# Attention, Mish MLP and SwiGLU MLP in one kernel: another order of work in the attention blocks at its start

## Chip, cores and metric

The kernel runs on one core of a Trainium2 chip. The metric is the device time of one execution in microseconds (us); a time quoted for a version is the median of several runs.

## The reference, cut to what matters

```python
# q, k, v: (4, 8, 576, 64)
scores = np.matmul(q, k.transpose(0, 1, 3, 2)) / np.sqrt(D)
# heads 0 to 3: the 32 positions up to the own one; heads 4 to 7: every 32nd position up to the own one
attn = softmax(np.where(mask, scores, -1e9))
x = np.matmul(attn, v)  # as (2304 tokens, 512)
h = x @ w_in            # 512 -> 2048
x = (h * np.tanh(softplus(h))) @ w_out
x = (silu(x @ w_gate) * (x @ w_val)) @ w_out2   # 512 -> 1536 -> 512
```

The weights come as 64-bit floats and are made into 32-bit ones on the chip.

## The kernel before, in words

**Attention** is cut into 24 steps: 4 batches, in each 3 steps of local heads (8 or 6 small score tiles of 64 queries by 96 keys) and 3 of strided heads (8 or 6 tiles of 64 by 64). One call of `at_pair` issues one *block*: parts of four steps at once, by the table `PAIR` of (function, lag). Block a holds, in the order of the table: loads (`at_load`), the transposes of step a-2 (`at_tr`, PE, line L394) with their copy out of PSUM (`at_copy`, first half on DVE, L404, second on ACT, L402), the sum's small addition and the normalisation of step a-1 (`at_add`, `at_norm`: POOL L374 and L382, DVE reciprocal L379), the product with v of step a-3 (`at_pv`, PE, L423), its split into a high part on ACT (`at_hi`, L81) and a low part on DVE (`at_lo`, L86), the scores of step a (`at_qk`, PE, L322), their masked maximum on DVE (`at_max`, L347) and their exponentials on ACT (`at_exp`, L363). The result of attention, x, lies in five chunks of 512 tokens as a pair `xh`, `xl`. Blocks are counted from 0; blocks 0 to 14 are issued by one loop, the later ones inside the matmuls of the MLP, at the places `PAIR_AT`.

**Between blocks** the loop issues, for block k: `KEEP[k]` idle matmuls on zeros (`spin`, L830), `WSTEPS[k]` steps of weight conversion, and the matmul steps `GROUPS[k]` of the first MLP. A step (n, f, kc) is three matmuls of 512 columns into PSUM tile f of chunk n, from slice kc of x: high by high, high weight by `xl`, low weight by high (`mm3`, L90; PE tile `h`). Slice kc belongs to head pair kc, so a slice becomes ready in the block whose `at_pv` finishes that pair.

**A weight tile** takes four conversion steps on DVE (L214, L217, L220, L223) and a square on ACT (L213) in between. When the four are done, the next block's `at_whi` rounds the high part on ACT (L81, tile `w`), and `at_wlo` at the end of that block takes the low part on DVE (L86, tile `w`). The third conversion step frees the raw buffer (two of them), so that the next raw tile can be loaded (`w_load`, 512 KB).

**Order.** Each engine takes its instructions in the order in which the code issues them. SP issues the loads in that order too. A load on the SP and ACT queues waits until the eighth one before it has landed.

Of the kernel before, what the change touches and what calls it, by code (L numbers as in the profile page):

```python
# [7 lines left out]
F32 = mybir.dt.float32  # L8
# [18 lines left out]
QW = S + 16  # L27
KW = S + STR
# [24 lines left out]
}  # L53
WSTEPS = (0, 0, 4, 0, 2, 2, 4, 2, 2, 2, 2, 2, 2, 2, 2)
WFILL = 4
PAIR_AT = (0, 13, 16, 19, 22, 25, 28, 31, 35, 40, 45, 49)
WF = 8
DO2 = 6

# [2 lines left out]
def local_strided_attention__mish_moe__swiglu_kernel(  # L62
# [10 lines left out]
    nc = tc.nc  # L73
    small = ctx.enter_context(tc.tile_pool(name="small", bufs=1))
    sb = ctx.enter_context(tc.tile_pool(name="sb", bufs=1))
# [9 lines left out]
    def split_lo(eng, lo, src, hi):  # L85
        eng.tensor_tensor(out=lo, in0=src, in1=hi.bitcast(F32), op=ALU.subtract)  # L86
# [10 lines left out]
    xh, xl, acc = {}, {}, {}  # L97
# [35 lines left out]
    def w_load():  # L133
        i = wpos[0]
        while i < len(wlist) and wlist[i][1] is None:
            i += 1
        if i >= late["first"] and late["raw"] is None:
            return
        if i < len(wlist):
            if i < late["first"]:  # L140
                raws[i] = sb.tile([128, 512], I64, tag="raw", name="raw", bufs=2)
            else:
                raws[i] = late["raw"][:, late["loads"] % 2]
                late["loads"] += 1
            nc.sync.dma_start(raws[i], wlist[i][1])
        wpos[0] = i + 1
# [124 lines left out]
    pairs = []  # L271
    steps, at_first, at_last = [], {}, {}
    for b in range(B):
        for first in (0, 2) if b < B - 1 else (2, 0):
# [18 lines left out]
    qk_t, v_t = {}, {}  # L293
    st = {}

    def load_qk(i, cuts=((0, QW + KW),)):
        b, hp = pairs[i]
        a = QK_SLOT[i]
        t = sb.tile([128, QW + KW], F32, tag=f"acc{a}", name="qk")
        for c0, c1 in cuts:  # L300
            nc.sync.dma_start(t[:, c0:c1], qk[4 * b + hp, :, c0:c1])
        qk_t[i] = t

    def load_v(s):
        b, first, g, part = steps[s]
        n = len(part) // 2
        k = 128 if first else LK
        t = sb.tile([128, 2, 4, 128], F32, tag="v", name="v", bufs=2)[:k, :, :n]
        src = (v_str if first else v_loc)[b, 2 * g:2 * g + 2, :, :n]
        nc.sync.dma_start(t, src.rearrange("x p n d -> p x n d"))  # L310
        for x in range(2):
            v_t[s, x] = t[:, x]
# [155 lines left out]
    def at_wlo(s):  # L468
        w_lo(nc.vector)
# [4 lines left out]
    def of(do, h):  # L474
        return lambda s: do(s, h)

    PAIR = [
        (at_load, 0),
        (of(at_tr, 0), -2),
        (of(at_copy, 0), -2),  # L480
        (at_add, -1),
        (at_norm, -1),
        (at_pv, -3),
        (at_v, -3),
        (at_hi, -3),
# [9 lines left out]
        (at_wlo, 0),  # L495
    ]
    SPLIT, EXP0, COPY1, EXP1 = 9, 11, 15, 16
    apos = [0]

    rest = []  # L500

    def at_rest():
        while rest:
            rest.pop(0)()

    def at_pair(split=False, later=()):
        at_rest()
        a = apos[0]
        if a < NS + 3:
            apos[0] += 1  # L510
            for x, (do, lag) in enumerate(PAIR):
                if 0 <= a + lag < NS:
                    if x in later:
                        held.append(lambda do=do, s=a + lag: do(s))
                    elif split and x >= SPLIT:
                        rest.append(lambda do=do, s=a + lag: do(s))
                    else:
                        do(a + lag)
# [303 lines left out]
    with tc.manual_schedule():  # L822
        nc.gpsimd.memset(wz, 0.0)

        def spin(n):
            if not n:
                return
            wp = ps.tile([128, 512], F32, tag="mm", name="wp", bufs=3)
            for _ in range(n):
                nc.tensor.matmul(  # L830
                    wp, lhsT=wz[:, :128], rhs=wz.unsqueeze(1).to_broadcast([128, 2, 256]), start=True, stop=True
                )

        spin(NWARM)
        load_qk(0, ((QW, QW + 416),))
        nc.scalar.dma_start(qk_t[0][:, :384], qk[0, :, :384])
        nc.scalar.dma_start(cst[:, :192], consts[:, :192])
        load_qk(1, ())
        nc.scalar.dma_start(qk_t[1][:, :192], qk[1, :, :192])
        for i, c0, c1 in ((0, 384, QW), (0, QW + 416, QW + KW), (1, QW, QW + 224)):  # L840
            nc.sync.dma_start(qk_t[i][:, c0:c1], qk[i, :, c0:c1])
        nc.sync.dma_start(cst[:, 192:], consts[:, 192:])
        w_load()
        for c0, c1 in ((192, QW), (QW + 224, QW + KW)):
            nc.sync.dma_start(qk_t[1][:, c0:c1], qk[1, :, c0:c1])
        load_v(0)
        load_qk(2)
        load_v(1)
        load_qk(3)
        w_load()  # L850
        nc.scalar.preload_act_table_set(EXP)

        NA = NQ * NCH
# [7 lines left out]

        for k in range(len(WSTEPS)):
            at_pair()
            spin(KEEP.get(k, 0))
            w_step(WSTEPS[k])
            for x in GROUPS.get(k, ()):
                g1_step(*x)
                if x == (1, 0, 3):
                    for f in range(QF):
                        act_m(0, (f,))  # L870
                        g_hi(0, f)
        MISH = (
            (lambda: act_m(1, (0, 1, 2)), lambda: g_lo(0, 0)),
            (lambda: g_lo(0, 1),),
            (lambda: g_lo(0, 2),),
            (),
            (lambda: at_wlo(0), lambda: g_lo(0, 3), lambda: w_step(WFILL), lambda: act_m(1, (3,)), act_m_end),
        )
# [3 lines left out]
        def fill():  # L882
            at_rest()
            if fills[0] in PAIR_AT:
                at_pair(apos[0] >= NS, () if fills[0] else LATER)
            for x in MISH[fills[0]] if fills[0] < len(MISH) else ():
                x()
            fills[0] += 1
            do(3 if len(todo) > 10 else 2 if len(todo) > DO2 else 1)

        g1s = [(1, 3, kc) for kc in range(4)]
        g1s += [(2, f, kc) for kc in range(4) for f in range(3)] + [(2, 3, kc) for kc in range(4)]
        wfill = [0]
        for n in range(1, 3):
# [16 lines left out]
        while apos[0] < NS + 3:  # L911
            at_pair()
# [177 lines left out]
```

## Time and profile before

| what | value |
| --- | --- |
| time, median of 3 runs | 892.99 us (891.73 to 895.02) |
| the profiled execution | 891.96 us, span 890.0 us |
| PE busy | 874.6 us, 98% |
| DVE, ACT, POOL busy | 584.1, 379.6, 136.5 us |
| chain that ended last, PE's share | 96% |

The page gives the busy time of each engine and cuts the span into 40 slices of 22 us; the trace gives single instructions with their start, and what ended the idle time before one. In the rows below, a time counts from the start of the span.

### The profile page before, as it was taken

How to read it: one execution, taken by the hardware profiler on the slowest of the kernel's cores; microseconds unless marked ns; L12 is line 12 of the kernel's file. 1: busy time of each engine (PE TensorE's matmuls, PEld its weight loads, DVE VectorE, ACT ScalarE, POOL GpSimd, SP SyncE). 2: the span in 40 equal slices, each digit the busy share in tenths (PEclk: the TensorE clock that was granted, in tenths of full speed). 3: DMA queues.
4: the chain of work that ended last, by engine and by line, in shares of the span. 5: the costliest groups of instructions: out<-in, count | busy, mean ns of one | idle time of the engine just before them, and what ended most of it. 6: DMA issues, size and time to landing. Idle time of an engine off the chain costs nothing.

```text
span 890.0 us, 14231 instructions
## 1 busy us (share of the span) xinstructions
PE 874.6 (98%) x5284; PEld 728.5 (82%) x5284; DVE 584.1 (66%) x1272; ACT 379.6 (43%) x940; POOL 136.5 (15%) x156
## 2 busy tenths in 40 slices
PE   7889999999999999999999999999999999999998
PEld 4677888888888888888888888888888888888886
DVE  5778776789676987776484897765445635333534
ACT  6679874254343534353343543342323412332230
POOL 2322320000000000000031330211314312111211
PEclk9999999999999999999999999999999999999999
DMA  9656623246532544342029789665260563553222
GB/s 268 217 182 185 210 82 119 95 145 210 189 119 95 197 182 142 112 149 94 25 85 365 258 323 344 237 256 205 103 236 24 190 240 120 208 189 131 106 95 95
DMA packets 49124, 151.90 MB, mean 171 GB/s; under 512 B 5024, under 2 KB 12704, under 8 KB 49056
## 3 DMA queue, kind: packets, MB, share of 16 engines
q1 hardware_dynamic: 48624, 150.61, 47.9%
q8 instruction: 42, 0.69, 0.3%
q10 hardware_dynamic: 432, 0.39, 0.1%
q14 instruction: 26, 0.21, 0.1%
HBM read 114.80 MB, written 36.18 MB: 170 GB/s over the span
## 4 chain that ended last, share of the span: by engine, by line
PE 96%; DVE 1%; DMA 1%; ACT 1%; POOL 0%; issue 0%; SPq 0%; ACTq 0%; POOLq 0%
PE y L90 22%; PE h L90 22%; PE o L90 17%; PE cXg L90 7%; PE cXv L90 7%; PE c L90 4%; PE cZv L90 4%; PE cZg L90 4%; PE xp L423 2%; PE cYv L90 2%; PE cYg L90 2%; PE sc L322 1%; PE tp L394 1%; DMA qk<-in_qk_dram 1%; ACT pt L363 1%; DVE pt L347 1%
## 5 line engine op out<-in xcount | busy, mean ns | idle before, releaser
L90 PE MATMUL y<-g,w 128*128 128x512 f32 (+1 forms) x960 | 202.8, 369 | 0.0
L90 PE MATMUL h<-xh,w 128*128 128x512 f32 (+1 forms) x640 | 189.6, 373 | 5.8 <-DVE w L86 3.5
L90 PEld LDWEIGHTS y<-g,w 128*128 128x128 f32 x960 | 166.8, 189 | 30.7 <-DVE w L86 0.4
L90 PE MATMUL o<-wr,fs 128*128 128x512 f32 x648 | 149.6, 389 | 0.0
L90 PEld LDWEIGHTS o<-wr,fs 128*128 128x128 f32 x648 | 121.3, 188 | 25.0
L90 PEld LDWEIGHTS h<-xh,w 128*128 128x128 f32 x640 | 116.3, 189 | 28.2 <-DVE w L86 4.7
L90 PE MATMUL h<-xl,w 128*128 128x512 f32 (+1 forms) x320 | 118.6, 371 | 1.4 <-DVE xl L86 1.4
L558 ACT ACTIVATE u<-h 128x512 f32<-128x512 f32 (+1 forms) x68 | 37.2, 548 | 142.3 <-PE h L90 142.3
L817 DVE TENSOR_TENSOR acc<-acc,o 128x512 f32<-128x512 f32 x90 | 61.4, 686 | 48.6 <-PE o L90 48.5
L86 POOL TENSOR_TENSOR fs<-k,fs 128x512 fp32r<-128x512 f32 x36 | 48.6, 1351 | 267.1 <-ACT fs L81 208.4
L90 PEld LDWEIGHTS h<-xl,w 128*128 128x128 f32 x320 | 60.5, 189 | 12.2 <-DVE xl L86 2.6
L86 DVE TENSOR_TENSOR g<-u,g 128x512 fp32r<-128x512 f32 (+1 forms) x80 | 51.1, 661 | 15.1 <-ACT g L81 15.1
L363 ACT ACTIVATE pt<-pt,sm 128x64 f32<-128x64 f32 (+1 forms) x160 | 55.7, 351 | 10.3 <-DVE sm L347 10.3
L81 ACT CAST fs<-k 128x512 fp32r<-128x512 f32 x36 | 22.4, 622 | 88.1 <-DVE k L772 37.6
L758 DVE TENSOR_TENSOR k<-cZg,k 128x512 f32<-128x512 f32 x12 | 8.3, 692 | 73.3 <-PE cZg L90 73.3
L90 PE MATMUL cXg<-T,wr 128*128 128x512 f32 x216 | 54.8, 389 | 0.0
L90 PE MATMUL cXv<-T,wr 128*128 128x512 f32 x216 | 54.8, 389 | 0.0
L86 POOL TENSOR_TENSOR B<-acc,B 128x512 fp32r<-128x512 f32 x6 | 8.3, 1390 | 301.2 <-ACT B L81 301.2
L81 ACT CAST ws<-wt 128x512 fp32r<-128x512 f32 x60 | 36.9, 615 | 36.5 <-DVE wt L223 29.2
L81 ACT CAST g<-u 128x512 fp32r<-128x512 f32 (+1 forms) x80 | 44.5, 574 | 15.2 <-PE y L90 15.1
L90 PEld LDWEIGHTS cXg<-T,wr 128*128 128x128 f32 x216 | 40.5, 188 | 8.5 <-DVE k L758 0.2
L90 PEld LDWEIGHTS cXv<-T,wr 128*128 128x128 f32 x216 | 40.5, 188 | 8.4
(102 smaller groups left out, 1316.5 us busy)
## 6 DMA issues: line engine op xcount, KB each, us to landing
raw<-in_w_dram SPq DMA_DIRECT2D x54, 512.0 KB, 3.6
wr<-wd_g_S SPq DMA_DIRECT2D x24, 512.0 KB, 7.2
wr<-wd_v_S SPq DMA_DIRECT2D x24, 512.0 KB, 7.4
wr<-wd_p SPq DMA_DIRECT2D x24, 512.0 KB, 5.1
wr<-wd_g_W SPq DMA_DIRECT2D x18, 512.0 KB, 6.3
wr<-wd_v_W SPq DMA_DIRECT2D x18, 512.0 KB, 7.0
qk<-in_qk_dram SPq DMA_DIRECT2D x14, 600.0 KB, 5.7
rawl<-in_w_dram SPq DMA_DIRECT2D x14, 512.0 KB, 6.3
```

What stands on the lines that cost most here:

```text
L81: nc.scalar.copy(hi, src)
L86: eng.tensor_tensor(out=lo, in0=src, in1=hi.bitcast(F32), op=ALU.subtract)
L90: nc.tensor.matmul(o, lhsT=lhs, rhs=rhs, start=first and i == 0, stop=last and i == 2, skip_group_check=more)
L322: nc.tensor.matmul(sc[h][x % 2 * 64:x % 2 * 64 + 64, x // 2 * w:(x // 2 + 1) * w], lhsT=t[64 * h:64 * h + 64, q0:q0 + 64], rhs=t[64 * h:64 ...
L347: nc.vector.tensor_tensor_reduce(pt[:, x], sc[h][:, t * w:(t + 1) * w], m, -0.125, 3.0e38, ALU.add, ALU.min, accum_out=sm[:, 0, x:x + 1],)
L363: nc.scalar.activation(out=pt[:, x], in_=pt[:, x], func=AF.Exp, scale=-1.0, bias=sm[:, 0, x:x + 1], accum_out=sm[:, 1, x:x + 1],)
L394: nc.tensor.transpose(tp[:, 128 * x:128 * x + 128], a, ident)
L423: nc.tensor.matmul(xp[64 * h:64 * h + 64, o:o + nq - skip], lhsT=vt[:, y % n, 64 * h:64 * h + 64], rhs=ts[:, c0 + skip:c0 + nq], start=Tru ...
L558: nc.scalar.activation(out=u, in_=p, func=AF.Mish)
L758: nc.vector.tensor_tensor(out=t, in0=p, in1=t, op=ALU.add)
L817: nc.vector.tensor_tensor(out=acc[c][:, t], in0=acc[c][:, t], in1=o, op=ALU.add)
```

## The change

Blocks 1 to 3 (`SC_FIRST`) are issued in another order: scores, maxima and exponentials (`SCORES`) come first, then the rest of the table. The loads of the third and fourth q and k are cut in two parts each, the part that the first step on them needs ahead of the rest, and the first two raw weight tiles move behind some of them. `WSTEPS` moves weight conversion: the sum stays 28, blocks 2 to 9 have 4, 0, 2, 2, 4, 2, 2, 2 steps before and 0, 4, 4, 4, 2, 2, 1, 1 now. `GROUPS` moves matmul steps between blocks 8 and 14, and one step past block 14; `PAIR_AT` and `MISH` follow by one place.

```diff
-    8: ((0, 0, 3), (0, 1, 3), (0, 3, 0)),
-    9: ((0, 2, 2), (0, 2, 3), (0, 3, 1)),
+    8: ((0, 0, 3), (0, 1, 3), (0, 2, 2)),
+    9: ((0, 2, 3), (0, 3, 0), (0, 3, 1)),
...
-    13: ((1, 0, 2), (1, 1, 2), (1, 2, 2)),
+    13: ((1, 2, 1), (1, 0, 2), (1, 1, 2)),
...
-WSTEPS = (0, 0, 4, 0, 2, 2, 4, 2, 2, 2, 2, 2, 2, 2, 2)
+WSTEPS = (0, 0, 0, 4, 4, 4, 2, 2, 1, 1, 2, 2, 2, 2, 2)
...
+SC_FIRST = (1, 2, 3)
...
+    SCORES = [9, 10, EXP0, 13, EXP1]
...
-            for x, (do, lag) in enumerate(PAIR):
+            order = list(range(len(PAIR)))
+            if a in SC_FIRST:
+                order = SCORES + [x for x in order if x not in SCORES]
+            for x in order:
+                do, lag = PAIR[x]
...
+        more_qk(1, ((192, QW), (QW + 224, QW + KW)))
+        load_qk(2, ((0, 448), (QW, QW + 448)))
+        load_v(0)
         w_load()
-        for c0, c1 in ((192, QW), (QW + 224, QW + KW)):
-            nc.sync.dma_start(qk_t[1][:, c0:c1], qk[1, :, c0:c1])
-        load_v(0)
-        load_qk(2)
         load_v(1)
-        load_qk(3)
+        more_qk(2, ((448, QW), (QW + 448, 2 * QW)))
+        load_qk(3, ((0, 288), (QW, QW + 288)))
         w_load()
+        more_qk(3, ((288, QW), (QW + 288, 2 * QW)))
...
-        g1s = [(1, 3, kc) for kc in range(4)]
+        g1s = [(1, 2, 3)] + [(1, 3, kc) for kc in range(4)]
```

SP, start of the program, before (the first four loads are the first parts of q and k 0 and 1, the fifth the rest of the constants; `raw` is a weight tile):

```order
L842 DMA cst<-in_consts_dram 128x288
L145 DMA raw<-in_w_dram 128x512
L845 DMA qk<-in_qk_dram 128x400
L845 DMA qk<-in_qk_dram 128x384
L310 DMA v<-in_v_loc_dram 96x2x384
L301 DMA qk<-in_qk_dram 128x1200
```

and now:

```order
L851 DMA cst<-in_consts_dram 128x288
L306 DMA qk<-in_qk_dram 128x400
L306 DMA qk<-in_qk_dram 128x384
L306 DMA qk<-in_qk_dram 128x448 x2
L314 DMA v<-in_v_loc_dram 96x2x384
L146 DMA raw<-in_w_dram 128x512
```

The raw tile has moved behind the second parts of q and k 1 (400 and 384 columns), the first parts of q and k 2 and the first v.

ACT, from its first exponentials to block 4, before (`pt` 128x96 are steps 0 to 2, 128x64 step 3 and on):

```order
L363 ACTIVATE pt,sm<-pt,sm 128x96 x15
L402 COPY ts<-tp 96x256
L363 ACTIVATE pt,sm<-pt,sm 128x96 x3
L213 ACTIVATE w<-raw 128x512
L81 CAST xh_68<-xp 128x384
L81 CAST w<-wtmp 128x512
L363 ACTIVATE pt,sm<-pt,sm 128x64 x4
L402 COPY ts<-tp 96x256
```

and now:

```order
L367 ACTIVATE pt,sm<-pt,sm 128x96 x18
L406 COPY ts<-tp 96x256
L367 ACTIVATE pt,sm<-pt,sm 128x64 x8
L82 CAST xh_68<-xp 128x384
L406 COPY ts<-tp 96x256
L214 ACTIVATE w<-raw 128x512
```

The exponentials of steps 0 to 3 now stand together, with one copy between them; the first weight's square and high part come after them.

DVE, from the last maximum of block 4 to the first copy of block 5, before:

```order
L347 ISA pt_364,sm_365<-sc_347,cst_66 128x64
L347 ISA sm_365 128x1
L214 TENSOR_SCALAR wtmp_395<-raw_111 128x512
L217 SCALAR_TENSOR_TENSOR wtmp_395<-raw_111,wtmp_395 128x512
L404 COPY ts_407<-tp_402 128x512
L379 RECIPROCAL sm_365<-sm_365 128x8
```

and now:

```order
L351 ISA pt_369,sm_370<-sc_352,cst_66 128x64
L351 ISA sm_370 128x1
L87 TENSOR_TENSOR w_311<-wtmp_310,w_311 128x512
L215 TENSOR_SCALAR wtmp_401<-raw_115 128x512
L218 SCALAR_TENSOR_TENSOR wtmp_401<-raw_115,wtmp_401 128x512
L221 SCALAR_TENSOR_TENSOR wtmp_401<-raw_115,wtmp_401 128x512
L224 SCALAR_TENSOR_TENSOR wtmp_401<-w_402,wtmp_401 128x512
L408 COPY ts_417<-tp_412 128x512
L383 RECIPROCAL sm_370<-sm_370 128x8
```

Three instructions more stand between block 4's maxima and block 5's copy: the first weight's low part and two more steps of the second weight.

## Rows read from the trace of the kernel before

**Rows 1.** Page: busy us, share of the span and instructions of each engine.

```profile
PE 874.6 (98%) x5284; PEld 728.5 (82%) x5284; DVE 584.1 (66%) x1272; ACT 379.6 (43%) x940; POOL 136.5 (15%) x156
```

**Rows 2.** Waits of PE, 0 to 150 us: total, times, longest.

```profile
PE h L90 <- DVE w L86: 3.5, 3, 1.2
...
PE h L90 <- DVE xl L86: 1.4, 3, 0.5
PE h L90 <- ACT w L81: 1.2, 2, 0.7
...
PE h L90 <- ACT u L556: 1.0, 1, 1.0
```

**Rows 3.** Windows: length, busy PE, PEld, DVE, ACT, POOL; clock, DMA share, GB/s.

```profile
3.00:4.00 1.00, 1.00 (x3) 0.15 (x1) 0.00 (x0) 0.40 (x1) 0.00 (x0) 1.00 1.05 352
5.00:10.00 5.00, 3.05 (x37) 1.44 (x33) 2.51 (x26) 3.86 (x21) 1.53 (x3) 1.00 0.96 265
19.05:47.06 28.01, 22.69 (x316) 16.39 (x318) 20.50 (x102) 19.38 (x94) 8.46 (x16) 0.94 0.68 219
33.00:34.00 1.00, 1.00 (x5) 0.66 (x3) 0.90 (x2) 0.00 (x0) 0.00 (x0) 0.50 0.00 0
140.00:800.00 660.00, 660.00 (x3228) 560.02 (x3227) 439.25 (x714) 254.73 (x467) 82.34 (x67) 1.00 0.49 176
```

**Rows 4.** Chain that ended last, at its start: start, us, what.

```profile
4.92 5.91 DMA qk<-in_qk_dram
```

**Rows 5.** Timeline of ACT and DVE, blocks 2 to 4 and 6: start, us, instruction.

```profile
12.44 0.38 ACT L363 ACTIVATE pt<-pt,sm 128x96 f32<-128x96 f32 x1 [1.78 <-DVE sm L347]
15.99 0.48 ACT L81 CAST xh<-xp 128x384 fp32r<-128x384 f32 x1 [0.46 <-PE xp L423]
17.18 0.35 ACT L363 ACTIVATE pt<-pt,sm 128x64 f32<-128x64 f32 x1 [0.19 <-DVE sm L347]
17.41 0.55 DVE L86 TENSOR_TENSOR xl<-xp,xh 128x384 fp32r<-128x384 f32 x1
19.05 0.68 DVE L404 COPY ts<-tp 96x512 f32<-96x512 f32 x1
20.11 0.57 ACT L81 CAST xh<-xp 128x128 fp32r<-128x128 f32 x3
31.56 0.42 DVE L214 TENSOR_SCALAR wtmp<-raw 128x512 int32<-128x512 int32 x1
34.34 0.56 DVE L404 COPY ts<-tp 128x384 f32<-128x384 f32 x1
```

**Rows 6.** Timeline of PE: starts of scores and transposes; nine MLP matmuls.

```profile
28.53 0.73 PE L322 MATMUL sc<-qk 64*64 64x96 f32 x24
33.46 0.84 PE L394 MATMUL tp<-cst,pt 128*128 128x128 f32 x3
35.76 0.73 PE L322 MATMUL sc<-qk 64*64 64x96 f32 x24
46.43 0.60 PE L394 MATMUL tp<-cst,pt 128*96 128x128 f32 x4
47.80 0.69 PE L322 MATMUL sc<-qk 64*64 64x64 f32 x32
52.65 0.60 PE L394 MATMUL tp<-cst,pt 128*96 128x128 f32 x4
54.03 0.69 PE L322 MATMUL sc<-qk 64*64 64x64 f32 x32
56.99 0.60 PE L394 MATMUL tp<-cst,pt 128*128 128x128 f32 x4
66.31 0.73 PE L322 MATMUL sc<-qk 64*64 64x96 f32 x24
69.92 0.60 PE L394 MATMUL tp<-cst,pt 128*96 128x128 f32 x4
89.65 2.34 PE L90 MATMUL y<-g,w 128*128 128x512 f32 x9
```

More of the change, by code (lines that the diff above doesn't have):

```diff
@@ L45 @@
     7: ((0, 0, 2), (0, 1, 2)),
[2 rows of a table removed]
[2 rows of a table added]
     10: ((0, 3, 2), (0, 3, 3), (1, 0, 0)),
[4 rows of a table removed]
[4 rows of a table added]
 }
-WSTEPS = (0, 0, 4, 0, 2, 2, 4, 2, 2, 2, 2, 2, 2, 2, 2)
+WSTEPS = (0, 0, 0, 4, 4, 4, 2, 2, 1, 1, 2, 2, 2, 2, 2)
 WFILL = 4
-PAIR_AT = (0, 13, 16, 19, 22, 25, 28, 31, 35, 40, 45, 49)
+PAIR_AT = (0, 14, 17, 20, 23, 26, 29, 32, 36, 41, 46, 50)
+SC_FIRST = (1, 2, 3)
 WF = 8
@@ L298, in load_qk, with more_qk @@
         a = QK_SLOT[i]
-        t = sb.tile([128, QW + KW], F32, tag=f"acc{a}", name="qk")
+        qk_t[i] = sb.tile([128, QW + KW], F32, tag=f"acc{a}", name="qk")
+        more_qk(i, cuts)
+    def more_qk(i, cuts):
+        b, hp = pairs[i]
         for c0, c1 in cuts:
-            nc.sync.dma_start(t[:, c0:c1], qk[4 * b + hp, :, c0:c1])
-        qk_t[i] = t
+            nc.sync.dma_start(qk_t[i][:, c0:c1], qk[4 * b + hp, :, c0:c1])
     def load_v(s):
@@ L839, in local_strided_attention__mish_moe__swiglu_kernel @@
         nc.scalar.dma_start(qk_t[1][:, :192], qk[1, :, :192])
-        for i, c0, c1 in ((0, 384, QW), (0, QW + 416, QW + KW), (1, QW, QW + 224)):
-            nc.sync.dma_start(qk_t[i][:, c0:c1], qk[i, :, c0:c1])
+        more_qk(0, ((384, QW), (QW + 416, QW + KW)))
+        more_qk(1, ((QW, QW + 224),))
         nc.sync.dma_start(cst[:, 192:], consts[:, 192:])
+        more_qk(1, ((192, QW), (QW + 224, QW + KW)))
+        load_qk(2, ((0, 448), (QW, QW + 448)))
+        load_v(0)
         w_load()
-        for c0, c1 in ((192, QW), (QW + 224, QW + KW)):
-            nc.sync.dma_start(qk_t[1][:, c0:c1], qk[1, :, c0:c1])
-        load_v(0)
-        load_qk(2)
         load_v(1)
-        load_qk(3)
+        more_qk(2, ((448, QW), (QW + 448, 2 * QW)))
+        load_qk(3, ((0, 288), (QW, QW + 288)))
         w_load()
+        more_qk(3, ((288, QW), (QW + 288, 2 * QW)))
         nc.scalar.preload_act_table_set(EXP)
@@ L872, in local_strided_attention__mish_moe__swiglu_kernel @@
         MISH = (
-            (lambda: act_m(1, (0, 1, 2)), lambda: g_lo(0, 0)),
-            (lambda: g_lo(0, 1),),
+            (lambda: g_lo(0, 0),),
+            (lambda: act_m(1, (0, 1, 2)), lambda: g_lo(0, 1)),
             (lambda: g_lo(0, 2),),
+            (),
             (),
```

6 rows, old and new, of the table GROUPS are left out of this document.

## Prediction

> **What bounds the kernel now.** First the page: PE is busy for 874.6 us [rows 1] of the 890.0 us span. Then the windows: from 140 to 800 us PE is busy for 660.00 of 660 us, at a granted clock of 1.00 [rows 3]. The change moves no PE work away, so there is nothing to win or lose there as long as DVE and ACT keep up. What is left is the start, with most of the 890.0 - 874.6 = 15.4 us of idle PE. Its waits there [rows 2]: 3.5 us in three waits for a weight's low part (`DVE w`), 1.2 us in two for its high part (`ACT w`), 1.4 us in three for the low part of x (`DVE xl`), 1.0 us for the copy of a full PSUM tile (`ACT u`).
>
> What they cost is more than that, since the pipeline empties and the clock falls, so I read it off block starts [rows 6]. Block 10 has no wait: from its scores (54.03) to the next transposes (56.99) 2.96 us with three matmul steps; its transposes and v products, 52.65 to 54.03, take 1.38. A step is three matmuls of 512 columns; nine take 2.34 with the tail of the last, so a step is 0.70, and two steps would make 2.26. From the scores of block 6 (28.53) to the transposes of block 10 (52.65) there are two blocks with two steps, two with three and three rounds of transposes and products: 2 x 2.26 + 2 x 2.96 + 3 x 1.38 = 14.6 us. It took 24.1: **9.5 us too long**. Block 6 alone took 28.53 to 33.46, 4.93 for 2.26, and at its end the granted clock was 0.50, the 1.2 GHz level [rows 3], after PE had been mostly waiting. Block 9 took 47.80 to 52.65, 4.85, so 1.9 too long. Block 13 took 66.31 to 69.92, 3.61, so 0.65 too long, and block 14 repeats it with some 0.8. All together 11 us: the most that the change can remove there.
>
> **The change part by part.** *Weights one block ahead.* Now the four conversion steps of the second and third weight end in blocks 4 and 5, their low parts in blocks 5 and 6, and the steps that use them stand in blocks 6 and 7: the waits in blocks 6 and 7 go. The fourth weight is ready at the end of block 8 and first used by the third step there, so two steps (1.4 us) cover it; the wait of block 9 goes with the full 1.9. The `ACT u` wait of block 8 goes, since no fourth PSUM tile is opened there.
>
> *Old slices first.* In blocks 13 and 14 the first step now reads a slice that is a block older: 0.65 + 0.8 = 1.5 us go. Blocks 7 and 8 still begin with a new slice; there a wait as in block 13, 0.65 each, stays. The step that left block 11 runs past block 14: the same work later, nothing.
>
> *The price is on DVE.* What was spread over blocks 2 to 8 now stands in 3 to 8, and DVE takes it in order: four steps and a low part ahead of a block's copy, behind which the transposed tiles, the maxima and the low part of x are queued, and PE waits for these. So DVE paces blocks 4 to 8, and I work this out from one row to another: the copy of block 4 (19.05 before) to the copy of block 9, at 47.06, right after the transposes at 46.43 [rows 5, 6]. DVE was busy for 20.50 of these 28.01 us [rows 3]. Now there are 13 conversion steps in it instead of 12, and four low parts instead of two: 20.50 + 0.45 + 2 x 0.60 = 22.2 us (0.60 for a low part is estimated from the 0.55 of the smaller `xl` with 384 columns [rows 5]). All else that DVE does there is as before.
>
> *Where that chain starts* depends on blocks 0 to 3. Before, the second parts of q and k 1 landed at 4.92 + 5.91 = 10.83 [rows 4], behind a 512 KB weight. At 265 GB/s [rows 3] that is 2.0 us, so now 8.9. The exponentials of step 2 began 1.6 us after the landing (12.44 [rows 5]); now 10.5. Since scores come first, ACT has them one after another: six of step 2 by about 0.37 (2.2), a copy (0.25), eight of step 3 by 0.335 (17.18 to 20.11 with one copy between, so 2.68): 15.6. Then the high part of x (0.48) and its low part on DVE (0.55), then four conversion steps, 31.56 to 34.34 = 2.8 with 0.2 of stalls inside [rows 5], so 2.6. Sum: 15.6 + 0.5 + 0.5 + 2.6 = **19.2** for the copy of block 4, where it was 19.05. The low bound is 18.6 (PE at full clock through block 2, so scores sooner), the high one 20.2 (PE at 1.2 GHz there, so the idle matmuls ahead of block 3's scores take an us more). I take 19.4, a little over the sum. So the early blocks win nothing by the clock; what they win is that a whole weight more has been made by then.
>
> *Sum.* Copy of block 9 at 19.4 + 22.2 = 41.6 instead of 47.06. PE needs some time of its own there (three steps in block 8 and two waits for a new slice), so I put its transposes at 41.8 instead of 46.43: 4.6 us earlier. Block 9: 1.9. Blocks 13 and 14: 1.5. Together **8.0 us**. DVE and ACT stay under PE's pace from block 10 on, since their work in those blocks is the same; one matmul step less in block 11 lets DVE pace it for half an us, which blocks 12 and 13 make good.
>
> *Transfers.* Two transfers of 600 KB become eight of 72 to 224 KB. The small ones at the start, 96 to 208 KB each, already moved 352 GB/s from 3 to 4 us, with the 16 engines busy all along [rows 3], and that is more than the 265 later; I cost the cut at nothing, as eight transfers in flight keep the engines fed. The Trainium skill speaks against it: "DMA: Bandwidth & Descriptors", section "Bandwidth", asks for 1 MiB or more in one transfer for 75% of peak; by that rule the cut would slow the queue just where step 4's scores wait. The 352 GB/s do not agree with it for this kernel, and the rule is kept as a rival.
>
> **The rivals.**
> 1. *The loads land no earlier*, because what counts is the slowest of 16 engines and not the bytes ahead. For it: a span of 5.91 us for 192 KB. Against: 512 KB less are queued. Then the copy of block 4 is at 21.2 and the gain is 8.0 - 1.8 = 6.2: 886.8.
> 2. *The clock.* PE is now idle before block 5's transposes (about 2 us: normalisation of step 3 after the copy at 19.4) and within block 5, where the third step waits for an `xl` that stands behind four conversion steps (1.3 us). Before, such a stretch took the clock to 0.50 for about 3 us [rows 3]. Transposes and products then took 33.46 to 35.76, 2.30 for 1.38 [rows 6], so work costs half as much again. If 3 us of work fall into it, waits that are there anyway (some 4 us in blocks 5 to 8) hide it. If it holds through block 8, 18 us of PE work cost 9 and hide 4: gain 3, 890. If it holds past block 10, with 27 us of work, it costs 13.5 - 4 = 9.5: **1.5 us slower than before**, 894.5. It decides from 24 us of work at the low level. Against it: no low stretch in the rows is that long.
> 3. *Transfers of this size are slow* (the rule above). Priced by rows: if each of the four small ones for steps 3 and 4 held the queue for half of the 2.0 us that 512 KB take, 4 us in all less 1.3 of slack before step 4's scores, the gain is 5.3: 887.7.
> 4. *Given back later:* between 76 and 100 us ACT has a table load, the Mish and the splits of two chunks in a row; if PE comes there earlier against ACT than now, it waits. Against: one matmul step more (0.7) now lies between block 14's scores and the first MLP product, about what the wait removed there was worth. Price 3 us, 888.
> 5. *The change doesn't do what it says:* DVE might pace blocks 4 to 8 as slowly as the waits did. That needs 27 us of DVE work for the 22.2 above; I see no such row.
>
> **How the numbers follow.** The sum against the profiled execution: 891.96 - 8.0 = 884.0. The median of the runs is 1.0 above that execution, so 892.99 - 8.0 = **885.0 us**. Chances: forecast 0.60; rival 1 0.14; rival 2 0.10, of which 0.04 past break-even; rival 3 0.05; rival 4 and 5 together 0.11. The range takes the bounds of the start (18.6 to 20.2, so a gain of 7.2 to 8.8), another 1.5 us for what runs of one kernel differ, and rivals 1, 3 and 4: 882.5 to 889.5. About 0.5% (4.5 us) can be told from no change here. Faster by more than that, below 888.5: nearly all of the forecast, rival 1, and most of rivals 3 and 4: 0.78. Within it: 0.18. Slower: 0.04.
>
> **What would show each step right or wrong.** In the profile of the changed kernel: scores of block 2 at about 9 us instead of behind the landing at 10.83; exponentials of steps 0 to 3 with hardly a gap, ending near 15.6; the DVE copy of block 4 near 19.4 and the one of block 9 near 41.6, with DVE busy nearly all the time between; no `DVE w` or `ACT w` wait of PE in blocks 6, 7 and 9; a new wait of PE for `xl` of more than 1 us in block 5; no wait in blocks 13 and 14; PE without idle time from there on. The forecast is wrong if DVE idles between 19 and 41 us for something I haven't seen, if the granted clock is low for more than 3 us after 16 us, or if new idle time of PE appears behind 76 us.

## The result, and the profile after

The changed kernel takes **884.12 us** (median of 4 runs, 883.4 to 884.3); the kernel before, run beside it, 892.36 us (4 runs, 891.61 to 895.02). The ratio is 0.9901, with a 95% interval of 0.9879 to 0.9923: faster by 1%, 8.2 us. The profiled execution has a span of 881.2 us against 890.0, so 8.8 us less.

Page of the changed kernel: the span, PE's busy time (answers to [rows 1]), its busy tenths and its clock in the 40 slices.

```profile
span 881.2 us, 14244 instructions
...
PE 870.6 (99%) x5284; PEld 726.6 (82%) x5284; DVE 583.3 (66%) x1272; ACT 379.8 (43%) x940; POOL 135.9 (15%) x156
...
PE   7999999999999999999999999999999999999998
...
PEclk9999999999999999999999999999999999999999
```

PE has as many instructions as before and is busy 4.0 us less. Most of that is work that ran at the lower clock and now runs at the full one: in the kernel before, the granted clock was low in two stretches (window: length, busy PE, PEld, DVE, ACT, POOL; clock, DMA share, GB/s).

```profile
11.00:15.00 4.00, 4.00 (x34) 2.44 (x34) 2.99 (x16) 2.56 (x14) 1.29 (x2) 0.57 1.04 282
...
31.00:36.00 5.00, 4.30 (x51) 3.43 (x55) 3.71 (x9) 1.65 (x8) 1.57 (x3) 0.66 0.45 143
```

From these mean clocks, 4 x 0.43 + 5 x 0.34 = 3.4 us of PE's full speed were missing there, an estimate. The other 4.8 us are idle time that is gone (15.4 to 10.6).

Waits of PE in the first 150 us, changed kernel (engine, tile and line, what it waited for: total, times, longest), which answers to [rows 2]:

```profile
PE h L91 <- DVE xl L87: 1.8, 3, 0.8
...
PE tp L398 <- POOL pt L386: 0.8, 2, 0.4
PE sc L326 <- DVE sm L351: 0.8, 2, 0.5
PE xp L427 <- DMA v<-in_v_loc_dram: 0.7, 1, 0.7
...
PE sc L326 <- DMA qk<-in_qk_dram: 0.6, 1, 0.6
```

The waits for `DVE w`, `ACT w` and `ACT u` are gone. `DVE xl` stays, now in blocks 5, 7 and 8 (0.75, 0.52, 0.50). Loads are waited for that the prediction did not name: q and k in block 4, v in block 5, and for 0.3 us v in block 7.

Timeline of PE, changed kernel (start, us, instruction): scores of block 2, scores of block 6, transposes and scores of block 9, transposes of blocks 10, 14 and 15. They answer to [rows 6].

```profile
8.35 0.84 PE L326 MATMUL sc<-qk 64*64 64x96 f32 x24 [0.52 <-DVE sm L351]
...
28.48 0.73 PE L326 MATMUL sc<-qk 64*64 64x96 f32 x24
...
40.99 0.60 PE L398 MATMUL tp<-cst,pt 128*96 128x128 f32 x4
...
42.37 0.69 PE L326 MATMUL sc<-qk 64*64 64x64 f32 x32
...
45.34 0.60 PE L398 MATMUL tp<-cst,pt 128*96 128x128 f32 x4
...
61.21 0.60 PE L398 MATMUL tp<-cst,pt 128*96 128x128 f32 x4
...
65.60 0.60 PE L398 MATMUL tp<-cst,pt 128*96 128x128 f32 x4
```

Block 6's scores start as before (28.48, was 28.53), but block 10's transposes come at 45.34 instead of 52.65. That stretch takes 16.9 us where it took 24.1. Block 15's transposes stand at 65.60; before, they stood here:

```profile
75.01 0.60 PE L394 MATMUL tp<-cst,pt 128*96 128x128 f32 x4
```

That is 9.41 us earlier. One matmul step (0.70) now comes later, so 8.7 is won by then: all of the 8.8 of the span. Behind it PE waits for nothing in either kernel.

Timeline of ACT and DVE, changed kernel: the high part of x in block 3, its low part, the first conversion step, DVE's copies of blocks 4, 8 and 9, and the first maximum of block 8. They answer to [rows 5].

```profile
14.78 0.46 ACT L82 CAST xh<-xp 128x384 fp32r<-128x384 f32 x1
...
15.27 0.56 DVE L87 TENSOR_TENSOR xl<-xp,xh 128x384 fp32r<-128x384 f32 x1 [1.57 <-ACT xh L82]
15.74 0.42 DVE L215 TENSOR_SCALAR wtmp<-raw 128x512 int32<-128x512 int32 x1
...
18.34 0.68 DVE L408 COPY ts<-tp 96x512 f32<-96x512 f32 x1
...
36.81 0.68 DVE L408 COPY ts<-tp 96x512 f32<-96x512 f32 x1
...
37.99 0.26 DVE L351 CUSTOM_DVE_ANT_0 pt<-sc,cst 128x96 f32<-128x96 f32 x1 [0.41 <-PE sc L326]
...
41.63 0.69 DVE L408 COPY ts<-tp 96x512 f32<-96x512 f32 x1 [1.09 <-PE tp L398]
```

From 18.34 to 36.81 no DVE row of this profile carries a wait: DVE sets the pace there. Only in block 8 does it wait for PE, for 0.41 and 1.09 us.

Windows of the changed kernel (length, busy PE, PEld, DVE, ACT, POOL; clock, DMA share, GB/s), which answer to [rows 3]:

```profile
3.00:4.00 1.00, 1.00 (x3) 0.15 (x1) 0.00 (x0) 0.40 (x1) 0.00 (x0) 1.00 1.08 373
...
5.00:10.00 5.00, 3.87 (x59) 2.28 (x60) 3.19 (x34) 4.64 (x26) 1.68 (x4) 1.00 0.96 253
...
11.00:15.00 4.00, 3.66 (x70) 2.61 (x70) 2.02 (x19) 4.00 (x24) 2.74 (x5) 1.00 1.08 253
...
18.34:41.63 23.29, 19.93 (x271) 14.38 (x272) 21.38 (x105) 19.18 (x85) 8.16 (x15) 1.00 0.85 283
...
140.00:800.00 660.00, 660.00 (x3229) 559.98 (x3228) 439.56 (x714) 252.52 (x463) 83.92 (x68) 1.00 0.49 176
```

The granted clock is 1.00 in each of them, and 140 to 800 us is what it was.

### The profile page after: what moved, and what is told of

It is laid out like the page before. It is cut to its first block, busy times and chain, and to the rows that moved or that the text cites. A ratio compares the mean times of both kernels' runs of the same rounds, so it can differ in the third digit from the quotient of the medians.

```text
span 881.2 us, 14244 instructions
## 1 busy us (share of the span) xinstructions
PE 870.6 (99%) x5284; PEld 726.6 (82%) x5284; DVE 583.3 (66%) x1272; ACT 379.8 (43%) x940; POOL 135.9 (15%) x156
## 4 chain that ended last, share of the span: by engine, by line
PE 96%; DVE 2%; ACT 2%; issue 0%; POOL 0%; DVEq 0%; ACTq 0%; POOLq 0%
PE y L91 23%; PE h L91 22%; PE o L91 17%; PE cXg L91 7%; PE cXv L91 7%; PE c L91 4%; PE cZv L91 4%; PE cZg L91 4%; PE xp L427 2%; PE cYv L91 2%; PE cYg L91 2%; ACT pt L367 1%; PE sc L326 1%; PE tp L398 1%; PE wp L839 0%; DVE pt L351 0%
## 5 line engine op out<-in xcount | busy, mean ns | idle before, releaser
L82 ACT CAST g<-u 128x512 fp32r<-128x512 f32 (+1 forms) x80 | 44.6, 575 | 15.6 <-PE y L91 15.4
```

The source lines that it names most:

```text
L82: nc.scalar.copy(hi, src)
```

## The experiments

Theory: DVE paces blocks 4 to 8, so what counts is when its chain starts (loads, order of scores) and how much stands in it; the moved weights take away PE's waits for `w`; the older slices are worth 1.5 us by themselves. The rivals: the loads alone explain it, the clock explains it, or the parts do something else than I had said. The first four runs undo one part of the change each; four more do one thing alone on the kernel before; the last four change DVE's load in the changed kernel. "Copy 4" and "copy 9" are DVE's copies of blocks 4 and 9, at 18.34 and 41.63 in the changed kernel. The first microseconds of the start differ by some 0.4 us from one profile to another, so less than 0.5 us in a span says nothing. The changed kernel's profile is an early one: it is the fastest of its four runs, and in the five profiles below whose blocks 0 to 3 are its own (slices undone, and the four runs on DVE's load) copy 4 stands at 18.75 to 18.87, not at 18.34. So a span or a copy compared with it can look up to 0.5 us too late; the medians beside the spans show this. Not tested are the loads alone on the kernel before, and the cut of the loads apart from their new order.

**Undone: scores first.**

```diff
-SC_FIRST = (1, 2, 3)
+SC_FIRST = ()
```

> The changed kernel, with blocks 1 to 3 in the old order again (scores not first). Theory (DVE paces blocks 4 to 8 from the copy of block 4 on, and scores first is what lets that copy come early): the exponentials of steps 1 to 3 stand behind copies and high parts again, the copy of block 4 comes 1 to 2 us later than 18.34, and the span grows by as much: 882.2 to 883.2 for 881.2. Rival (the earlier loads alone do it, the order of blocks 1 to 3 is indifferent): copy of block 4 within 0.4 of 18.34, span within 0.5 of 881.2.

885.29 us (885.03 to 885.45), ratio to the kernel before 0.9929 (0.9912 to 0.9946); span 883.2, 2.0 more than with it; median 1.2 more. Copy 4 at 19.36, copy 9 at 43.20. So the order of the scores is worth 1 to 2 us here. At the chain's start it is 1.0 against the changed kernel's profile and 0.5 to 0.6 against the five others with its start. The chain takes 23.84 instead of 23.29, but that is not the order's doing as far as the rows show: PE waits 0.95 for a late v in block 7, and DVE 0.46 behind it, as in a profile that keeps the order (1.02 and 0.54, in the run with more on DVE in blocks 9 to 12).

**Undone: weights one block ahead.**

```diff
-    8: ((0, 0, 3), (0, 1, 3), (0, 2, 2)),
-    9: ((0, 2, 3), (0, 3, 0), (0, 3, 1)),
+    8: ((0, 0, 3), (0, 1, 3), (0, 3, 0)),
+    9: ((0, 2, 2), (0, 2, 3), (0, 3, 1)),
...
-WSTEPS = (0, 0, 0, 4, 4, 4, 2, 2, 1, 1, 2, 2, 2, 2, 2)
+WSTEPS = (0, 0, 4, 0, 2, 2, 4, 2, 2, 2, 2, 2, 2, 2, 2)
```

> The changed kernel, with the old conversion steps (WSTEPS) and the old matmul steps of blocks 8 and 9. Theory (most of the gain is the waits for weights in blocks 6, 7 and 9 and the copy of a full tile in block 8): these waits come back, the stretch from the scores of block 6 to the transposes of block 10 is 22 to 24 us instead of the 16.9 of the changed kernel, and of 8.8 us gain in the span 2 to 4 are left: 886 to 888. Rival (scores first and the loads carry the gain): the span stays within 2 us of 881.2.

893.06 us (891.74 to 896.26), ratio 1.0021 (1.0006 to 1.0036); span 890.3, so 9.1 more. The waits for `DVE w` (3.5), `ACT w` (1.2) and `ACT u` (1.0) are back as expected, and the stretch from the scores of block 6 (31.82) to the transposes of block 10 (54.41) takes 22.6 us, inside the 22 to 24 of the theory. But the theory left 2 to 4 us of gain and there is none: block 6's scores come 3.3 us later than in the changed kernel (28.48). DVE's and PE's timelines of this run show what I had missed, and the windows what followed:

```profile
13.49 0.43 DVE L215 TENSOR_SCALAR wtmp<-raw 128x512 int32<-128x512 int32 x1 [2.06 <-DMA raw<-in_w_dram]
...
16.08 0.22 DVE L351 CUSTOM_DVE_ANT_0 pt<-sc,cst 128x64 f32<-128x64 f32 x1
```

```profile
18.98 0.78 PE L398 MATMUL tp<-cst,pt 128*96 128x128 f32 x4 [3.88 <-POOL pt L386]
```

```profile
15.00:19.00 4.00, 0.12 (x2) 0.02 (x1) 2.91 (x20) 2.57 (x15) 0.90 (x2) 1.00 0.94 309
...
22.00:26.00 4.00, 4.00 (x44) 2.46 (x38) 2.88 (x22) 3.19 (x19) 0.83 (x2) 0.50 0.82 270
```

By the old table four conversion steps end block 2, ahead of block 3's maxima in DVE's order. The raw tile, now loaded later, is waited for (2.06); the first maximum of block 3 starts at 16.08, where the changed kernel has it at 11.76. PE has nothing to do from 15 to 19 us (0.12 busy), and then the clock is at 0.50, its 1.2 GHz level. So the moved weights do two things: they take the waits for `w` out of blocks 6 to 9, and they keep block 2 clear, without which the new loads and the new order lose.

**Undone: old slices first.**

```diff
-    13: ((1, 2, 1), (1, 0, 2), (1, 1, 2)),
-    14: ((1, 2, 2), (1, 0, 3), (1, 1, 3)),
+    13: ((1, 0, 2), (1, 1, 2), (1, 2, 1)),
+    14: ((1, 0, 3), (1, 1, 3), (1, 2, 2)),
```

> The changed kernel, with the new slice of x first again in blocks 13 and 14 and the old one last; nothing else is moved. Theory: the two waits for the low part of x come back (0.5 us each and the restart of the pipeline), block 13 takes 3.6 us from scores to transposes instead of 2.90 and block 14 3.7 instead of 3.04: span 1.3 to 1.5 us more, 882.6. Rival (DVE paces these blocks anyway, so the wait only moves): span within 0.4 of 881.2, with new waits of PE in blocks 12 to 16.

885.14 us (884.11 to 885.55), ratio 0.9926 (0.9910 to 0.9942); span 882.8, 1.6 more; median 1.0 more. The transposes of blocks 13, 14 and 15 of this run:

```profile
57.61 0.49 PE L398 MATMUL tp<-cst,pt 128*128 128x128 f32 x3
...
62.73 0.60 PE L398 MATMUL tp<-cst,pt 128*96 128x128 f32 x4
...
67.82 0.60 PE L398 MATMUL tp<-cst,pt 128*96 128x128 f32 x4
```

Blocks 13 and 14 take 5.12 and 5.09 us; in the changed kernel both take 4.39 (61.21 to 65.60 for block 14). That is 1.4 us, each time a wait for `xl` (0.48, 0.46) and what follows from it.

**Undone: the loads.**

```diff
+        w_load()
...
-        load_qk(2, ((0, 448), (QW, QW + 448)))
...
-        w_load()
+        load_qk(2)
...
-        more_qk(2, ((448, QW), (QW + 448, 2 * QW)))
-        load_qk(3, ((0, 288), (QW, QW + 288)))
+        load_qk(3)
...
-        more_qk(3, ((288, QW), (QW + 288, 2 * QW)))
```

> The changed kernel, with the old order of loads: q and k of the third and fourth pair in one piece each, the raw weight ahead of the second parts of q and k 1. Theory: scores of block 2 start at about 10.9 us instead of 8.35, the chain behind them moves by 2 to 2.5 us, and the span is 883 to 883.7 instead of 881.2. Rival (what bounds blocks 2 and 3 is ACT's exponentials, and the loads have slack): span within 0.7 of 881.2.

888.09 us (887.85 to 888.27), ratio 0.9961 (0.9946 to 0.9975); span 886.0, 4.8 more, and median 4.0 more: in kind what the theory said, and about twice its size. PE's timeline of this run, blocks 2 and 3, and its window:

```profile
11.26 1.36 PE L326 MATMUL sc<-qk 64*64 64x96 f32 x24 [3.48 <-DMA qk<-in_qk_dram]
12.54 1.51 PE L398 MATMUL tp<-cst,pt 128*96 128x128 f32 x6
13.85 1.37 PE L839 MATMUL wp<-wz 128*128 128x512 bf16 x4
15.15 0.69 PE L326 MATMUL sc<-qk 64*64 64x64 f32 x32
```

```profile
11.00:15.00 4.00, 3.75 (x34) 2.69 (x34) 1.85 (x14) 2.05 (x11) 0.42 (x1) 0.57 1.04 276
```

The scores of block 2 come 2.9 us later (11.26 against 8.35), and then the clock is low (mean 0.57 from 11 to 15 us, behind a wait of PE of 3.48): transposes, idle matmuls and scores up to block 3's, which take 2.66 us in the changed kernel (8.35 to 11.01), take 3.89. Copy 4 is at 22.46, copy 9 at 45.71, both 4.1 late; the chain between them has its usual length. That the clock makes a part of the 4 us is read from this one profile and not shown by the times: of the four runs, the one with a mean granted clock of 1.000 took 888.07 us, the three at 0.996 to 0.998 took 887.85 to 888.27.

**The weights alone, on the kernel before.**

```diff
-    8: ((0, 0, 3), (0, 1, 3), (0, 3, 0)),
-    9: ((0, 2, 2), (0, 2, 3), (0, 3, 1)),
+    8: ((0, 0, 3), (0, 1, 3), (0, 2, 2)),
+    9: ((0, 2, 3), (0, 3, 0), (0, 3, 1)),
...
-WSTEPS = (0, 0, 4, 0, 2, 2, 4, 2, 2, 2, 2, 2, 2, 2, 2)
+WSTEPS = (0, 0, 0, 4, 4, 4, 2, 2, 1, 1, 2, 2, 2, 2, 2)
```

> The kernel before, with the new conversion steps (WSTEPS) and the new matmul steps of blocks 8 and 9 alone. Theory (DVE paces blocks 4 to 8 once the weights are one block ahead, and its chain starts later here, since scores don't come first and the loads are the old ones): copy of block 4 at 20 to 21 us, copy of block 9 some 23 us behind it at 43 to 44 instead of 47.06, block 9 without its wait: span 4 to 5.5 us below 890.0, so 884.5 to 886. Rival (without the early scores the moved conversions only push the wait to other places): span within 2 us of 890.0.

887.37 us (885.82 to 890.02), ratio 0.9948 (0.9931 to 0.9965); span 884.9, so 5.1 less, as expected. Copy 4 at 19.76, copy 9 at 43.49: 0.7 later and 3.6 earlier than before. Of the parts run alone this one gains most.

**The slices alone, on the kernel before.**

```diff
-    11: ((1, 1, 0), (1, 2, 0), (1, 0, 1)),
-    12: ((1, 1, 1), (1, 2, 1)),
-    13: ((1, 0, 2), (1, 1, 2), (1, 2, 2)),
-    14: ((1, 0, 3), (1, 1, 3), (1, 2, 3)),
+    11: ((1, 1, 0), (1, 2, 0)),
+    12: ((1, 0, 1), (1, 1, 1)),
+    13: ((1, 2, 1), (1, 0, 2), (1, 1, 2)),
+    14: ((1, 2, 2), (1, 0, 3), (1, 1, 3)),
...
```

`PAIR_AT`, `MISH` and the step past block 14 follow, as in the change.

> The kernel before, with the new matmul steps of blocks 11 to 14 alone (old slice of x first, one step past block 14). Theory: blocks 13 and 14 lose 0.65 to 0.8 us each, span 1.3 to 1.5 us below 890.0: 888.6. Rival (given back behind block 14, where ACT is busy without a gap): span within 0.4 of 890.0, with new waits of PE behind 76 us.

890.90 us (888.33 to 892.96), ratio 0.9981 (0.9966 to 0.9995). In the profile blocks 13 and 14 take 4.40 and 4.39 us instead of 5.11 and 5.09: the 1.4 of the theory. Yet its span is 891.0, over that of before, and the windows say why:

```profile
31.00:36.00 5.00, 4.65 (x63) 3.62 (x63) 3.09 (x9) 1.64 (x8) 2.00 (x3) 0.66 0.46 144
...
38.00:42.00 4.00, 3.80 (x32) 2.90 (x32) 1.96 (x5) 0.98 (x4) 0.74 (x1) 0.57 0.46 151
...
51.00:56.00 5.00, 4.41 (x30) 3.36 (x31) 2.03 (x4) 2.74 (x12) 0.24 (x1) 0.66 0.29 107
```

Besides the low stretch at 31 to 36 us, which the kernel before has too, this execution has two more (the kernel before has 1.00 in both windows), in blocks that the edit does not touch. The term is read from its blocks, not from this span. Runs with the same mean granted clock agree with it: at 0.996, 890.38 to 891.17 us (4 runs) against 891.65 to 893.45 for the kernel before (11 runs).

**Scores first alone, on the kernel before.**

```diff
+SC_FIRST = (1, 2, 3)
...
-            for x, (do, lag) in enumerate(PAIR):
+            order = list(range(len(PAIR)))
+            if a in SC_FIRST:
+                order = SCORES + [x for x in order if x not in SCORES]
+            for x in order:
+                do, lag = PAIR[x]
```

> The kernel before, with scores first in blocks 1 to 3 alone. Theory (what ends block 6 and the blocks behind it is the weight's low part, and scores first doesn't move that conversion forward by much): span 0 to 1.5 us below 890.0, and the waits of blocks 6, 7 and 9 are all there. Rival (scores first carries the gain): span 4 us or more below 890.0.

894.70 us (893.71 to 895.85), ratio 1.0022 (1.0007 to 1.0037): a little slower, where I had expected a little faster. The conversion of block 2 stands ahead of block 3's maxima here as well; the window from 22 to 26 us shows the same low clock (0.52) as in the run with the old weights. The edit that is worth 1 to 2 us beside the moved weights costs some 2 without them.

**The clock in block 6.** Six more matmuls, which the step after them overwrites, on the kernel before, to keep PE busy where the clock fell:

```diff
+        for _ in range(6 if (n, f, kc) == (0, 2, 0) else 0):
+            nc.tensor.matmul(
+                h_ps[n, f][:, :nt], lhsT=w[:, 0, x * 128:(x + 1) * 128], rhs=xh[c][:, kc], start=True, stop=True
+            )
```

> The kernel before, with six more matmuls of 512 columns at the start of step (0, 2, 0) in block 6, where PE waits for the weight's low part; they write what the step's first matmul overwrites. Theory (part of what blocks 6 and 7 lose is the granted clock of 0.50 behind that wait): the matmuls lie in the wait, the clock stays at 1.00 from 28 to 36 us, and the transposes and products of block 7 take 1.5 us instead of 2.30: span 1 to 1.8 us below 890.0. Rival (the clock falls all the same, or the matmuls delay what stands behind them): span within 0.5 of 890.0 or up to 1.4 above it.

891.54 us (889.73 to 892.24), ratio 0.9981 (0.9966 to 0.9996); span 890.2 against 890.0, which is what the rival said. Two windows of this run:

```profile
31.00:36.00 5.00, 4.35 (x69) 3.36 (x67) 4.62 (x19) 3.17 (x15) 1.55 (x3) 1.00 0.41 128
...
38.00:42.00 4.00, 4.00 (x51) 3.10 (x54) 1.48 (x4) 0.77 (x2) 1.54 (x3) 0.57 0.75 246
```

The low stretch of block 6 is gone (transposes to scores of block 7 take 1.49 us instead of 2.30), and another stands one block on, where transposes to scores take 2.42 us instead of 1.35. What the clock alone costs is not told by this run. It does tell that the low stretch is not tied to one block. In both kernels it stands behind a wait of PE for a weight's low part (1.17 us before, 1.12 here), but not every such wait brings one: behind the 1.13 us that PE waits in block 7, the kernel before keeps 1.00 from 36 to 42 us.

**More on DVE where it paces:** the copy twice in blocks 4 to 7, 2.6 us of DVE work.

```diff
+                if s + 2 in (4, 5, 6, 7):
+                    nc.vector.tensor_copy(ts, tp)
```

> The changed kernel, with the DVE copy out of PSUM made twice in blocks 4 to 7: 4 x 0.60 = 2.4 us more of DVE work. Theory (DVE paces blocks 4 to 8): the copy of block 9 comes 1.3 to 2.4 us later than 41.63, and the span grows by as much: 882.5 to 883.6. Rival (PE or the loads pace these blocks): copy of block 9 and span within 0.5 us.

886.45 us (886.11 to 886.50), ratio 0.9936 (0.9919 to 0.9953); 2.3 over the median of the changed kernel, 3.5 over its span; the span, 884.7, lies above the theory's 882.5 to 883.6. DVE's copies of blocks 4, 8 and 9 in this run:

```profile
18.75 0.68 DVE L408 COPY ts<-tp 96x512 f32<-96x512 f32 x1
...
39.99 0.68 DVE L408 COPY ts<-tp 96x512 f32<-96x512 f32 x1
44.78 0.69 DVE L408 COPY ts<-tp 96x512 f32<-96x512 f32 x1 [1.07 <-PE tp L398]
```

From the copy of block 4 to that of block 8 it takes 21.24 us against 18.47 (18.34 to 36.81): what was added comes back in full (each second copy takes some 0.7 in DVE's order, not the 0.60 of the estimate). Another 0.4 of the span is the later start. From block 8 to block 9 nothing changes (4.79 against 4.82), since PE paces that block.

**More on DVE where it should not matter:** the same in blocks 9 to 12.

```diff
+                if s + 2 in (9, 10, 11, 12):
+                    nc.vector.tensor_copy(ts, tp)
```

> The changed kernel, with the same copy made twice in blocks 9 to 12 instead: the same 2.4 us of DVE work. Theory (PE paces from block 9 on, DVE idles about 0.5 to 1 us in each block): span within 0.5 us of 881.2. Rival (DVE paces all of the blocks): span 1.3 to 2.4 us more.

884.86 us (884.54 to 885.20), ratio 0.9919 (0.9904 to 0.9934). The span, 883.3, is 2.1 more than the changed kernel's, which taken by itself is the rival's range. But block 9's transposes stand at 42.02 already, 1.0 late before any added copy: 0.4 is the later start, and in block 7 PE waits 1.02 for v and DVE 0.54 behind it. From there to block 15's it takes 25.39 us against 24.61: 0.8 of the 2.6 added. Blocks 9 to 11 and 14 do not feel it; 12 and 13 lose 0.5 and 0.3; they stand at and behind the two blocks with only two matmul steps (11 and 12). The theory allowed 0.5, so it holds for these blocks but for that place.

**Less on DVE:** the weights' low parts of blocks 4 to 6 on POOL.

```diff
-        w_lo(nc.vector)
+        w_lo(nc.gpsimd if s in (4, 5, 6) else nc.vector)
```

> The changed kernel, with the weights' low parts of blocks 4 to 6 on POOL instead of DVE: 3 x 0.60 = 1.8 us less on DVE, 3 x 1.35 more on POOL, which idles most of these blocks. Theory (DVE paces): copy of block 9 comes 0.8 to 1.8 us earlier than 41.63 and the span is 879.4 to 880.4. Rival (POOL becomes the bound: the normalisation queues behind the low part, and the transposes wait for it): span the same or up to 1 us more.

884.22 us (883.98 to 884.51), ratio 0.9912 (0.9897 to 0.9927): nothing gained where the theory wanted 0.8 to 1.8 us; span 882.3, 1.1 more than the changed kernel's. DVE's and POOL's timelines of this run:

```profile
21.25 1.22 DVE L215 TENSOR_SCALAR wtmp<-raw 128x512 int32<-128x512 int32 x1
...
27.16 1.66 DVE L218 SCALAR_TENSOR_TENSOR wtmp<-raw,wtmp 128x512 int32<-128x512 int32 x1
```

```profile
20.93 1.27 POOL L87 TENSOR_TENSOR w<-wtmp,w 128x512 fp32r<-128x512 f32 x1
...
26.73 1.54 POOL L87 TENSOR_TENSOR w<-wtmp,w 128x512 fp32r<-128x512 f32 x1
```

In the changed kernel the same two DVE instructions, of the same weights:

```profile
21.36 0.41 DVE L215 TENSOR_SCALAR wtmp<-raw 128x512 int32<-128x512 int32 x1
...
27.09 0.69 DVE L218 SCALAR_TENSOR_TENSOR wtmp<-raw,wtmp 128x512 int32<-128x512 int32 x1
```

Three low parts of 0.69 leave DVE, but the conversion step beside each of them grows by 0.81, 0.97 and 0.68 us (the third 1.10 instead of 0.42), together 2.5. Each ends 0.3 to 0.6 us after POOL's instruction does, as if DVE stood still until POOL is done. The time did not move because DVE's chain did not get shorter (copy 4 to copy 8: 19.09 us), not because DVE does not pace. The outcome is the rival's, but the rows give another reason for it: POOL is not the bound, it sits idle for 2.3 us before the normalisations in blocks 5 and 6 and waits for DVE.

**The same, with matmul steps one place later,** so that PE doesn't wait for a new slice in blocks 7 and 8:

```diff
-    5: ((0, 0, 0), (0, 1, 0), (0, 0, 1), (0, 1, 1)),
-    6: ((0, 2, 0), (0, 2, 1)),
-    7: ((0, 0, 2), (0, 1, 2)),
...
+    5: ((0, 0, 0), (0, 1, 0), (0, 0, 1)),
+    6: ((0, 1, 1), (0, 2, 0)),
+    7: ((0, 2, 1), (0, 0, 2)),
...
```

> The changed kernel, with the low parts of blocks 4 to 6 on POOL as in the run beside it, and the matmul steps of blocks 5 to 11 one place later, so that blocks 7 and 8 too begin with an old slice of x. Theory: the waits for the low part of x in blocks 7 and 8 (0.52 and 0.50 us, and the restart) go, and PE no longer ends block 8: 0.7 to 1.3 us less than that run, span 878.2 to 879.6. Rival (DVE still paces through block 8, so nothing is won by PE's order): span within 0.4 of that run.

883.87 us (883.20 to 884.05), ratio 0.9907 (0.9892 to 0.9922); span 882.0, 0.3 less than without the shift. Copy 9 comes 1.3 us earlier than in that run (41.45), with one matmul step (0.70) less done by then. PE's waits for `xl` in blocks 7 and 8 shrink from 0.57 and 0.50 to 0.37 and nothing, but PE now waits 1.11 (0.40 without the shift) for the normalised tiles ahead of block 7's transposes, and almost nothing is won: PE only does later what it did there while DVE paced. I found no version that is clearly faster than the changed kernel.

## Why the prediction was right, step by step

The time was forecast at 885.0 (882.5 to 889.5) and is 884.1; the gain was forecast at 8.0 us and is 8.2 in the medians, 8.8 in the spans. By blocks:

| term | forecast | measured |
| --- | --- | --- |
| chain's start, copy of block 4 | 19.4 | 18.34 |
| chain, copy of block 4 to copy of block 9 | 22.2 | 23.29 |
| copy of block 9 | 41.6 | 41.63 |
| transposes of block 9 earlier by | 4.6 | 5.44 |
| block 9 | 1.9 | 1.87 |
| blocks 13 and 14 | 1.5 | 1.42 |

- **What bounds it.** Right: 140 to 800 us did not change, and the gain is complete by block 15.
- **DVE paces blocks 4 to 8.** Right: no wait of DVE's between 18.34 and 36.81, and added DVE work comes back in full there and not in blocks 9 to 11. In the kernels with the new weights and the same DVE work there, copy 4 to copy 9 takes nearly one length: 23.29 us (changed), 23.55 (slices last), 23.84 (no scores first), 23.25 (old loads), 23.73 (weights alone) and 23.91 (more on DVE in blocks 9 to 12), whatever the start between 18.34 and 22.46.
- **The size of that chain, and of its start, are the two terms mis-sized,** by 1.1 each, in opposite directions, so that copy 9 came out right by luck (41.63, forecast 41.6). The start lies below even the low bound of 18.6; the other profiles with this start, at 18.75 to 18.87, lie inside. In the 23.29 us DVE is busy for 21.38, less than the 22.2 worked out. The rest, which I did not count into the chain, is 1.50 us of waiting for PE in block 8 and 0.4 of gaps.
- **The step from copy 9 to the gain is wrong by 0.8,** and this is why the forecast of 8.0 falls short of the 8.8 in the spans. I put the transposes of block 9 at 41.8, to give PE 0.2 of its own behind the copy at 41.6. But the copy reads these transposes and stands behind them: by 0.63 us before (46.43 and 47.06) and by 0.64 now (40.99 and 41.63). A copy at 41.6 would have meant transposes at 41.0, 5.4 earlier instead of 4.6, and a gain of 8.8.
- **The start.** The steps were right in kind (block 2's scores at 8.35, forecast about 9; the exponentials of steps 0 to 3 without a gap; high part, low part and four conversion steps from 14.78 to 18.34, 3.6 us as summed). The exponentials end 0.8 us sooner than 15.6 (0.3 to 0.4 in the profiles with copy 4 at 18.75 to 18.87): block 2's scores are held up by DVE's maxima (`sm`) and not by the landing, and ACT has no gap from there on.
- **"The early blocks win nothing by the clock"** was too low. The clock was 0.57 from 11 to 15 us before and is 1.00 now. With the old loads it drops at 11 us in the changed kernel too and copy 4 is 4.1 us later, not 1.8. So my rival 1 would have cost about twice its price; how much of that the clock makes is open.
- **What the weights do.** Half of it: the waits for `w` in blocks 6, 7 and 9 went, worth 5.1 us alone. That they also keep block 2 clear of a conversion, and that without this scores first costs time, I had not seen. The parts do not add up: undoing one costs 2.0, 9.1, 1.6 and 4.8 us of span, 17.5 together, of a gain of 8.8 (in the medians 1.2, 8.9, 1.0 and 4.0, of 8.2).
- **Waits that were forecast.** `xl` in block 5: 0.75, forecast over 1 (1.49 with the slices undone, 1.45 with more on DVE in blocks 9 to 12, where v comes in time for block 5). Blocks 7 and 8: 0.52 and 0.50, forecast 0.65. None in blocks 13 and 14: right. The 2 us of idle PE ahead of block 5's transposes were 0.43, as idle matmuls and the scores of block 4 fill it. Not forecast: 0.6, 0.7 and 0.3 us for late loads in blocks 4, 5 and 7, off the path here, since DVE has no wait there. The one in block 7 is close to it: where it grows to 0.95 and 1.02 us in other profiles, DVE waits 0.46 and 0.54 behind it.
- **Rival 2 (clock)** did not come: the clock stayed at 1.00. **Rival 3 (small transfers)** did not come at its price of 2.7 us, but it is not excluded in a small size, since no run undoes the cut alone. From 5 to 10 us, when cut transfers are under way, the queues moved 253 GB/s, and 265 with whole ones before [rows 3]; step 4's scores did wait 0.56 us for q and k, unseen behind DVE's chain. The 373 GB/s from 3 to 4 us belong to the first loads of 96 to 208 KB, which are the same in both kernels, since SP issues the next ones from 4.03 us on:

```profile
4.03 1.75 SPq L306 DMA_DIRECT2D qk<-in_qk_dram  x4
```

The 1 MiB rule of the Trainium skill ("DMA: Bandwidth & Descriptors", section "Bandwidth") is not put to the test by the cut: whole and cut loads are both below 1 MiB. That loads of 96 to 208 KB together move 352 and 373 GB/s shows only that such a size is not slow by itself here. **Rival 4** (given back later): no wait behind 76 us. **Rival 5:** the chain would have had to be 27 us.

## What to carry to other kernels

Find the engine that paces a stretch and follow it from one of its own instructions to the same one some blocks on: that length held within 0.7 us while the start moved by 4 us, and it told what added instructions cost. Bringing the scores forward paid here only when the conversion that stood ahead of the next maxima, and the load that it waits for, moved too; so test parts together as well as one by one. Work moved to a neighbouring engine was not free where the two met in time: read the durations of the instructions beside it.

## What the runs showed of the hardware

**DVE and POOL.** A DVE instruction that ran beside a POOL `TENSOR_TENSOR` stretched from 0.41 to 1.22 and from 0.69 to 1.66 us, and ended shortly after POOL's. The Trainium skill ("SBUF — State Buffer", section "Who interferes with whom") has the two engines share a pair of ports, which one instruction holds to its end; it counts `tensor_scalar` among the DVE instructions that can take the pair, and says that one with two inputs in SBUF, as the second has here, contends with a POOL instruction that reads SBUF. These rows agree.

**The clock.** In kernels with PE waits in blocks 2 to 9, stretches of low clock stand at other places in other profiles (11 to 15 and 31 to 36 us in the kernel before; with the slices alone also 38 to 42 and 51 to 56, in blocks with the same instructions). In the kernel before, the time goes with them: of 49 runs beside these experiments, the 7 with a mean granted clock of 1.000 took 889.63 to 891.52 us, the 3 with 0.992 took 894.37 to 895.10. The changed kernel's 4 runs (0.998 to 1.000) lie between 883.4 and 884.3. So by an estimate from these medians (890.04 at 1.000, and 884.12) about 6 us of its gain stand at equal clock, and some 2 come from stretches that no longer occur. Its time also looks steadier: a spread of 0.9 us in those 4 runs, against 3.4 in the 4 of the kernel before beside them.
